# Weighted sums one step further behind the scores in the first ten units of a sigmoid-attention and top-1 MoE kernel

## The chip, the cores and the metric

The kernel runs on one core of a Trainium2 chip. The metric is the device time of one execution in microseconds (us); lower is better. Three runs of the kernel before gave 771.38 us in the median (771.14 to 772.06).

## What is computed

The reference, cut to what matters:

```python
def _attn_ref(q, k, v):                      # 8 batches, 12 heads, 448 tokens, 64 wide, float32
    scores = q @ k.transpose(0, 1, 3, 2) / sqrt(64) - log(448)
    return sigmoid(scores) @ v
def _moe_ref(x, w_gate, w1, w2):             # x: 3584 tokens x 768, 8 experts, hidden 1024
    expert_idx = argmax(x @ w_gate, axis=1)
    gate_w = softmax(x @ w_gate)[expert_idx]
    for e in range(8):
        out[mask_e] = gate_w * (relu(x[mask_e] @ w1[e]) @ w2[e])
```

## The kernel before, in words

**Units and steps.** The 48 pairs of heads (`g`; six to a batch) are taken two at a time as 24 units, `u`. A unit has seven steps, one per chunk `c` of 64 keys, and `s = 7 * u + c` counts the steps, 0 to 167. `scores(s)` (line 752) multiplies the keys of one chunk with the queries of both pairs, two heads to a pair, each head in a 64 x 64 quarter of TensorE; the result is two PSUM tiles `sc`, 128 x 448. They come from a pool of four, `ps_sc`, which is used in turn. `squash` puts the sigmoid of each into an SBUF tile `at` (eight of them) on ScalarE, line 750. `weighted(s)` (line 773) multiplies `at` with the values and adds into one PSUM tile `av` per pair over the seven steps of a unit, line 784. In the trace a float32 matmul of a quarter has two records, so the scores of one step, or its sums, are eight weight loads and eight matmuls. I call that a half-step.

**Two stages.** Up to step `START = 70` only attention runs, in rounds: each even `s` is one round, in which `weigh_to` emits some weighted sums, then the gate work that is due, then the DVE transposes of finished units (`turn_tokens`), then `score_to(s + 2)` the scores of two steps, then `copy_tokens` the ACT copies `xf` of finished units. From step 70 on, MoE matmuls (lines 243 and 266) fill the time between bursts of attention.

The rounds are these lines (948 to 955):

```python
if s % 2 == 0:
    weigh_to(min(s - 1, (done_av // ST + 1) * ST))
    if done_av and done_av % ST == 0:
        summed.setdefault(done_av // ST - 1, s)
    stages_early(s)
    turn_tokens()
    score_to(s + 2 if s else LEAD + 1)
    copy_tokens()
```

So a round never runs over the end of a unit: it has one, two or three steps of sums against two of scores.

**Gate work.** `stages_early` calls `gate_a(b)` two steps after the round in which the last unit of batch `b` was summed. `gate_a` (line 287) multiplies the six `xf` of the batch with the gate weights into `psg`, a tile of the same pool of four as the scores, and VectorE copies it out to `logits` (line 298). The fourth score tile after `psg` takes the same PSUM tile, so it waits for that copy. Later pieces (`early_b`, `early_c`, ...) stand at fixed steps; `early_c` ends in `ri`, from which SyncE (SP) reads which batch's tokens to load (`raw`, line 581).

**Into the MoE.** `SPLITS` names the steps at which the six column blocks of the first batch's tokens are split into a high and a low part on VectorE: a transpose (594), a cast (595) and a subtraction `xl` (598). `FIRST` names the steps at which the first weights are split: ScalarE casts `w1h` (161), GpSimd subtracts for `w1l` (162). `READY` turns the next keys and queries with VectorE (`turn`, 699), loads keys and values from GpSimd's queue (`load_values`, 687 and 691) and queries from SP's (667).

The order on each engine is the order in which this code emits; no scheduler moves anything here.

Of the kernel before, what the change touches and what calls it, by code (L numbers as in the profile page):

```python
# [24 lines left out]
def tile_sigmoid_attention_top1_moe(  # L25
# [263 lines left out]
    def gate_a(b):  # L289
        psg = small_ps(b, "psg")  # L290
        for t in range(KD):
            for h in range(2):
                n = t % 2 * 2 + h
                nc.tensor.matmul(
                    psg[32 * n : 32 * (n + 1), :GH], wg[:, t], wholes[b, t][:, h * GH : (h + 1) * GH],
                    start=(t < 2), stop=(t >= KD - 2),
                )
        nc.vector.tensor_copy(logits_0 if b == 0 else logits, psg[:, :GH])
# [290 lines left out]
    def split_tokens(n, t, high):  # L589

        xh = xpool.tile([P, S], F32R, tag="xh", name=f"xh_{n}_{t}")
        xl = xpool.tile([P, S], F32R, tag="xl", name=f"xl_{n}_{t}")
        whole = xpool.tile([P, S], F32, tag="whole", bufs=2, name=f"whole_{n}_{t}")
        nc.vector.transpose(whole.rearrange("p (j s) -> p j s", s=32), raws[n][:, :, t, :])
        high(xh, whole)
        low_parts.append((xl, whole, xh.bitcast(F32)))
        if n == 0:
            nc.vector.tensor_sub(*low_parts.pop())
        elif t > 0:
            nc.vector.tensor_sub(*low_parts.pop(0))  # L600
            if t == KD - 1:
                nc.vector.tensor_sub(*low_parts.pop(0))
        xch[n, t] = (xh, xl)
# [14 lines left out]
    def keep_tokens():  # L618

        while to_keep:  # L620
            b, n, xt = to_keep.pop(0)
            rows = x_tok[b * S : (b + 1) * S].rearrange("(j r) (i f) -> i r j f", r=32, i=4)
            nc.sync.nop()
            for i in range(4):
                put = nc.sync.dma_start(
                    rows[i][:, :, n * KH * 32 : (n + 1) * KH * 32],
                    xt[32 * i : 32 * (i + 1)].rearrange("r j t s -> r j (t s)"),
                )
                for got in taken:
                    tc.declare_no_dep(put.ins, got.ins, reason="the slots read earlier batches' tokens")  # L630
# [114 lines left out]
    ST = KC  # L745
# [26 lines left out]
    def weighted(s):  # L772
        u, c = divmod(s, ST)
        two = [2 * u + n for n in range(2)]
        for g in two:
            if c == 0:
                if u % 2 == 0 and s < START - ST:
                    psv[g] = ps_moe.tile([P, 512], F32, tag="moe", name=f"av_{g}")
                else:
                    psv[g] = ps_av.tile([P, 512], F32, tag="av", name=f"av_{g}")  # L780
            at = ats.pop((g, c))
            for h in range(2):
                rows = quarter(g, h)
                nc.tensor.matmul(  # L784
                    psv[g][OWN[1 - h if g == CROSS else h], :S], ops[g, "v"][rows, c, :], at[rows], start=(c == 0), stop=(c == KC - 1)
                )
        if c == KC - 1:
            for g in two:
                pv = psv.pop(g)
                if g not in BY_ROWS:  # L790
                    summed_up.append((g, pv))
                to_copy.append((g, pv))
# [4 lines left out]
    def turn_tokens():  # L797
        while summed_up:
            tokens(*summed_up.pop(0))

    def copy_tokens():
        while to_copy:
            g, pv = to_copy.pop(0)
            xf = xpool.tile([P, S], F32, tag="xf", bufs=6, name=f"xf_{g}")
            if g in BY_ROWS:
                to, frm = xf.rearrange("d (p c) -> d p c", c=KC), pv[:, :S].rearrange("d (c p) -> d p c", c=KC)
                if g == CROSS:
                    for own, other in zip(OWN, OWN[::-1]):
                        nc.vector.tensor_copy(to[own], frm[other])
                else:  # L810
                    nc.scalar.copy(to, frm)
                tokens(g, xf)
            else:
                nc.scalar.copy(xf, pv[:, :S])
            wholes[divmod(g, NP)] = xf

    WARM, K_POOL, BY_ROWS = 33, 22, (0, 1, 3)
    START = 70
    LOADS = (START - 15, START - 12, START - 9, START - 7, START - 5)
    FIRST = (START - 3, START - 1, START - 1)  # L820
    SPLITS = (START - 11, START - 10, START - 9, START - 8, START - 4, START - 3)
    PB = NP // 2 * ST
    MIX = (7, 7)

# [3 lines left out]
        2: lambda u: (turn(2 * u + 3, "k"), load_pair(2 * u + 5)),  # L828
        3: lambda u: (turn(2 * u + 3, "q"), load_values(2 * u + 3)),
    }  # L830
    BURST = 4

    def attention():

# [23 lines left out]
        done_av = done_sc = 0  # L858

        def weigh_to(n):  # L860
            nonlocal done_av
            while done_av < min(n, N_ST):
                weighted(done_av)
                done_av += 1

        def score_to(n):
            nonlocal done_sc
            while done_sc < min(n, N_ST):
                scores(done_sc)
                done_sc += 1  # L870
# [52 lines left out]
        summed = {}  # L923

        def stages_early(s):
            for b in range(B):
                if summed.get((b + 1) * NP // 2 - 1) == s - 2:
                    gate_a(b)
            for w in PLACES.get(s, ()):
                stage(*w)  # L930

        def stages_late(s):
            u, i = divmod(s, ST)
            b, r = divmod(s - PB, PB)
            if r == (BURST if b < B - 1 else 1) and (b + 1) * PB >= START:
                gate_a(b)
            for w in PLACES.get(s, ()):
                stage(*w)

        for s in range(N_ST + 11):  # L940
            u, i = divmod(s, ST)
            a = u * ST
            if s in LOADS:
                wts.load(LOADS.index(s) + 1)
            if s in FIRST:
                wts.ahead(FIRST.index(s) + 1)
            if s < START:
                if s % 2 == 0:
                    weigh_to(min(s - 1, (done_av // ST + 1) * ST))
                    if done_av and done_av % ST == 0:  # L950
                        summed.setdefault(done_av // ST - 1, s)
                    stages_early(s)
                    turn_tokens()
                    score_to(s + 2 if s else LEAD + 1)
                    copy_tokens()
            elif s == START:
                weigh_to(a)
                turn_tokens()
                score_to(a + 2)
                copy_tokens()  # L960
            yield s, MIX[0]
            keep_tokens()
            if s >= START:
                b, r = divmod(s - 3 * PB, PB)
                b += 1
                stages_late(s)
                if i == BURST:
                    for n in range(ST):
                        score_to(a + n + 3)
                        weigh_to(a + n + 1)  # L970
                        turn_tokens()
                        if n == ST - 1:
                            copy_tokens()
                        if r == PB - ST + BURST and n < KD:
                            split_tokens(b, n, nc.scalar.copy if n in (1, 4) else nc.vector.tensor_copy)
            if i in READY and s < N_ST:
                READY[i](u)
            if s in SPLITS:
                split_tokens(0, SPLITS.index(s), nc.vector.tensor_copy)
            yield s, MIX[1]  # L980
# [21 lines left out]
    for s, n in attention():  # L1002
        if s >= START:
            more(n)
# [362 lines left out]
```

## Time and profile before

| what | value |
|---|---|
| median of three runs | 771.38 us (771.14 to 772.06) |
| the profiled execution, its own time | 771.24 us |
| its span, first to last instruction | 769.4 us |
| mean granted TensorE clock | 1.00 of 2.4 GHz |
| TensorE matmul busy | 762.8 us, 99% |
| VectorE, ScalarE, GpSimd busy | 378.2, 382.2, 349.1 us |
| DMA | 125.67 MB, mean 163 GB/s |

A busy TensorE says only that a matmul is in flight; whether it goes at its full rate is seen from how many weight loads and matmuls start in a stretch. PEld is TensorE's weight-load row: it shows when each matmul's turn comes, and what it waited for. SPq and POOLq are the queues from which SyncE and GpSimd issue DMAs. In a timeline a bracket gives the idle time of that engine before the row and what ended it.

### The profile page before, as it was taken

Reading aid. Unit: us, or ns where it says so; the run is one execution under the profiler, and the core shown is the slowest. Engines: PE = TensorE matmul, PEld = TensorE weight load, DVE = VectorE, ACT = ScalarE, POOL = GpSimd, SP = SyncE. Lnnn points to the kernel's source line nnn. Section 1 sums busy time; section 2 is a strip of 40 time slices with the busy share of each in tenths; the row PEclk is TensorE's granted clock in tenths of the full one; section 3 lists DMA queues with packets and bytes.
Section 4 is the critical chain, followed back from the end, with each engine's and each line's share of the span. In section 5 each row is a group of like instructions: output and inputs, shape, how many; then the busy total and the mean of one; then the engine's idle time right before and its main releaser. Section 6 shows DMA issues by size and latency. Waiting matters only on the chain. (4 is left out here: it accounts for less than half of the span.)

```text
span 769.4 us, 15492 instructions
## 1 busy us (share of the span) xinstructions
PE 762.8 (99%) x5585; PEld 589.3 (77%) x5585; DVE 378.2 (49%) x790; ACT 382.2 (50%) x686; POOL 349.1 (45%) x342
## 2 busy tenths in 40 slices
PE   9999999999999999999999999999999999999997
PEld 5655547678687696876967769678689999999996
DVE  5433678375253751628415474244746392244443
ACT  6878676644526545364344552545523333445451
POOL 8665526245353151531705407044266654764351
PEclk9999999999999999999999999999999999999999
DMA  9786898896678665694575966566087454656671
GB/s 231 166 180 148 177 243 177 189 217 149 157 162 192 147 154 120 160 242 99 134 184 110 218 149 168 129 185 151 24 217 173 142 142 107 204 154 172 199 222 38
DMA packets 309921, 125.67 MB, mean 163 GB/s; under 512 B 208158, under 2 KB 305358, under 8 KB 309840
## 3 DMA queue, kind: packets, MB, share of 16 engines
q1 hardware_dynamic: 303632, 112.19, 61.6%
q0 software_dynamic: 5632, 11.53, 5.4%
q8 instruction: 45, 0.74, 0.5%
q10 hardware_dynamic: 576, 0.92, 0.4%
q14 instruction: 36, 0.29, 0.1%
HBM read 102.49 MB, written 22.49 MB: 162 GB/s over the span
## 5 line engine op out<-in xcount | busy, mean ns | idle before, releaser
L750 ACT ACTIVATE at<-sc,bias_s 128x448 f32<-128x448 f32 x336 | 190.7, 633 | 106.9 <-PE sc L768 106.2
L162 POOL TENSOR_TENSOR w1l<-wst,w1h 128x768 fp32r<-128x768 f32 x72 | 132.8, 1852 | 210.5 <-ACT w1h L161 207.9
L162 POOL TENSOR_TENSOR w2l<-wst,w2h 128x512 fp32r<-128x512 f32 x84 | 106.9, 1296 | 134.7 <-ACT w2h L161 134.6
L768 PE MATMUL sc<-qt,kt 64*64 64x448 f32 x1344 | 162.0, 543 | 0.0
L784 PE MATMUL av<-at,vn 64*64 64x448 f32 x1344 | 160.1, 536 | 0.0
L243 PE MATMUL ps<-xh,w1h 128*128 128x448 f32 x336 | 124.3, 370 | 0.0
L243 PE MATMUL ps<-xh,w1l 128*128 128x448 f32 x336 | 123.3, 367 | 0.0
L243 PE MATMUL ps<-xl,w1h 128*128 128x448 f32 x336 | 123.3, 367 | 0.0
L266 PE MATMUL ps<-hh,w2l 128*128 128x448 f32 x336 | 123.3, 367 | 0.0
L266 PE MATMUL ps<-hl,w2h 128*128 128x448 f32 x336 | 123.2, 367 | 0.0
L266 PE MATMUL ps<-hh,w2h 128*128 128x448 f32 x336 | 122.6, 365 | 0.0
L768 PEld LDWEIGHTS sc<-qt,kt 64*64 64x64 f32 x1344 | 75.3, 188 | 59.0 <-issue 46.5
L784 PEld LDWEIGHTS av<-at,vn 64*64 64x64 f32 x1344 | 57.5, 133 | 64.0 <-issue 53.8
L161 ACT CAST w2h<-wst 128x512 fp32r<-128x512 f32 x108 | 64.5, 620 | 75.7 <-PE ps L266 63.3
L250 ACT ACTIVATE hh<-ps 128x448 fp32r<-128x448 f32 x56 | 30.5, 545 | 138.1 <-PE ps L243 125.3
L279 DVE TENSOR_TENSOR ps<-ps,gt 128x448 f32<-128x448 f32 x42 | 40.7, 970 | 87.0 <-PE ps L266 84.7
L612 DVE STREAM_TRANSPOSE xt<-av 128x448 f32<-128x448 f32 x45 | 26.5, 626 | 95.3 <-PE av L784 95.3
L251 DVE SCALAR_TENSOR_TENSOR hl<-ps,hh 128x448 fp32r<-128x448 f32 x56 | 34.4, 614 | 76.5 <-ACT hh L250 67.0
L243 PEld LDWEIGHTS ps<-xh,w1h 128*128 128x128 f32 x336 | 63.1, 188 | 9.4 <-issue 4.4
L266 PEld LDWEIGHTS ps<-hh,w2l 128*128 128x128 f32 x336 | 65.2, 194 | 6.6 <-issue 3.5
L266 PEld LDWEIGHTS ps<-hl,w2h 128*128 128x128 f32 x336 | 65.2, 194 | 6.2 <-issue 3.2
L266 PEld LDWEIGHTS ps<-hh,w2h 128*128 128x128 f32 x336 | 65.2, 194 | 3.2
(215 smaller groups left out, 916.5 us busy)
## 6 DMA issues: line engine op xcount, KB each, us to landing
wst<-in_moe_w_dram SPq DMA_DIRECT2D x72, 384.0 KB
wst<-in_moe_w_dram SPq DMA_DIRECT2D x54, 512.0 KB
x_tok<-xt SPq DMA_DIRECT2D x64, 168.0 KB
qn<-in_q_dram SPq DMA_DIRECT2D x180, 56.0 KB
raw<-x_tok SPq DMA_DIRECT2D x28, 336.0 KB
out_dram<-ob SPq DMA_DIRECT2D x84, 112.0 KB
kn<-in_k_dram SPq DMA_DIRECT2D x104, 56.0 KB
kn<-in_k_dram POOLq DMA_DIRECT2D x76, 56.0 KB, 4.1
```

Source lines behind the costliest of these rows:

```text
L161: nc.scalar.copy(hi, st)
L162: eng.tensor_tensor(lo, st, hi.bitcast(F32), op=ALU.subtract)
L243: nc.tensor.matmul(ps[:, :S], a[:, ws], b_, start=(t == 0 and n == 0), stop=(t == KD - 1 and n == 2))
L250: nc.scalar.activation(hh[:, :S], ps[:, :S], AF.Relu)
L251: nc.vector.scalar_tensor_tensor(hl[:, :S], ps[:, :S], 0.0, hh[:, :S].bitcast(F32), op0=ALU.max, op1=ALU.subtract)
L266: nc.tensor.matmul(ps[:, :S], a, b_, start=(j == 0 and n == 0), stop=(j == KF - 1 and n == 2))
L279: nc.vector.tensor_tensor(by_gate, by_gate, gate_rows[b], op=ALU.mult)
L612: nc.vector.transpose(xts[b][:, :, t, :], pv[:, :S].rearrange("p (j s) -> p j s", s=32))
L750: nc.scalar.activation(at, ps[:, :S], AF.Sigmoid, bias=bias_s, scale=SCALE)
L768: nc.tensor.matmul(ps[quarter(g, h), :S], ks, ops[g, "q"][own], start=True, stop=True)
L784: nc.tensor.matmul(psv[g][OWN[1 - h if g == CROSS else h], :S], ops[g, "v"][rows, c, :], at[rows], start=(c == 0), stop=(c == KC - 1))
```

## The change

`BEHIND = 2` replaces the rule for the rounds before `START`: round `s` sums up to step `s - 3`, thus always the two steps `s - 4` and `s - 3`, also across the end of a unit. `summed` is filled by a loop, since the end of a unit may now lie within a round. The sixth block of tokens is split at step 68 instead of 67.

```diff
-    SPLITS = (START - 11, START - 10, START - 9, START - 8, START - 4, START - 3)
+    SPLITS = (START - 11, START - 10, START - 9, START - 8, START - 4, START - 2)
...
-    BURST = 4
+    BURST, BEHIND = 4, 2
...
-                    weigh_to(min(s - 1, (done_av // ST + 1) * ST))
-                    if done_av and done_av % ST == 0:
-                        summed.setdefault(done_av // ST - 1, s)
+                    weigh_to(s - BEHIND)
+                    while len(summed) < done_av // ST:
+                        summed[len(summed)] = s
```

What it does to the order shows at two places. The first is TensorE around `psg_2`, the gate matmuls of the third batch, at the end of the first stage (in the names the number after `sc`, `av` and `xf` is the pair, the next one the chunk). Before:

```order
L784 MATMUL av_19_1791<-at_19_1_1749,vn_19_1626 64x448 x2
L294 MATMUL psg_2_1798<-xf_12_1381,wg_98 32x224 x2
L294 MATMUL psg_2_1798<-xf_13_1383,wg_98 32x224 x2
L294 MATMUL psg_2_1798<-xf_14_1603,wg_98 32x224 x2
L294 MATMUL psg_2_1798<-xf_15_1605,wg_98 32x224 x2
L294 MATMUL psg_2_1798<-xf_16_1761,wg_98 32x224 x2
L294 MATMUL psg_2_1798<-xf_17_1763,wg_98 32x224 x2
L768 MATMUL sc_18_3_1812<-qt_18_1570,kt_18_1558 64x448 x2
L768 MATMUL sc_19_3_1813<-qt_19_1624,kt_19_1612 64x448 x2
L768 MATMUL sc_18_4_1822<-qt_18_1570,kt_18_1558 64x448 x2
L768 MATMUL sc_19_4_1823<-qt_19_1624,kt_19_1612 64x448 x2
```

and with the change:

```order
L784 MATMUL av_19_1780<-at_19_2_1753,vn_19_1626 64x448 x2
L294 MATMUL psg_2_1839<-xf_12_1457,wg_98 32x224 x2
L294 MATMUL psg_2_1839<-xf_13_1459,wg_98 32x224 x2
L294 MATMUL psg_2_1839<-xf_14_1603,wg_98 32x224 x2
L294 MATMUL psg_2_1839<-xf_15_1605,wg_98 32x224 x2
L294 MATMUL psg_2_1839<-xf_16_1805,wg_98 32x224 x2
L294 MATMUL psg_2_1839<-xf_17_1807,wg_98 32x224 x2
L768 MATMUL sc_18_5_1853<-qt_18_1566,kt_18_1554 64x448 x2
L768 MATMUL sc_19_5_1854<-qt_19_1624,kt_19_1612 64x448 x2
L768 MATMUL sc_18_6_1863<-qt_18_1566,kt_18_1554 64x448 x2
L768 MATMUL sc_19_6_1864<-qt_19_1624,kt_19_1612 64x448 x2
```

`psg_2` now stands after the scores of steps 0 to 67 and the sums of 0 to 65, where it stood after 0 to 65 and 0 to 64: three half-steps later. In both, the built program makes the last score tile shown (`sc_19_4`, now `sc_19_6`), the fourth behind `psg_2`, wait for VectorE.

The second place is VectorE at the same time, from the turn of pair 20's keys on. Before:

```order
L699 STREAM_TRANSPOSE kt_1719<-kn_1560 128x448
L612 STREAM_TRANSPOSE xt_1_1581<-av_1635 128x14x32
L612 STREAM_TRANSPOSE xt_1_1581<-av_1638 128x14x32
L699 STREAM_TRANSPOSE qt_1770<-qn_1565 128x448
L699 STREAM_TRANSPOSE kt_1776<-kn_1614 128x448
L298 COPY logits<-psg_1798 128x224
L699 STREAM_TRANSPOSE qt_1832<-qn_1619 128x448
L594 STREAM_TRANSPOSE whole_4_1839<-raw_1429 128x448
L595 CAST xh_4_1837<-whole_4_1839 128x448
L598 TENSOR_TENSOR xl_4_1838<-whole_4_1839,xh_4_1837 128x448
```

and with the change:

```order
L699 STREAM_TRANSPOSE kt_1715<-kn_1556 128x448
L699 STREAM_TRANSPOSE qt_1755<-qn_1561 128x448
L699 STREAM_TRANSPOSE kt_1761<-kn_1614 128x448
L612 STREAM_TRANSPOSE xt_1_1581<-av_1635 128x14x32
L612 STREAM_TRANSPOSE xt_1_1581<-av_1638 128x14x32
L699 STREAM_TRANSPOSE qt_1814<-qn_1619 128x448
L594 STREAM_TRANSPOSE whole_4_1821<-raw_1418 128x448
L595 CAST xh_4_1819<-whole_4_1821 128x448
L598 TENSOR_TENSOR xl_4_1820<-whole_4_1821,xh_4_1819 128x448
L298 COPY logits<-psg_1839 128x224
```

The copy of `psg` stood ahead of the turn of pair 21's queries and of the split of the fifth token block; now both stand ahead of it.

## Rows read from the trace of the kernel before

**Rows 1.** The page, part 1: engines' busy time, share, instructions.
```profile
PE 762.8 (99%) x5585; PEld 589.3 (77%) x5585; DVE 378.2 (49%) x790; ACT 382.2 (50%) x686; POOL 349.1 (45%) x342
```
**Rows 2.** Busy time by stretch; in brackets the instructions; at the end clock, DMA share, GB/s.
```profile
43.80:76.90 33.10, 33.10 (x354) 17.26 (x352) 11.15 (x20) 26.31 (x49) 18.32 (x31) 1.00 0.74 160
86.00:110.10 24.10, 24.10 (x256) 12.39 (x256) 22.05 (x73) 19.24 (x38) 12.48 (x21) 1.00 0.98 207
```
**Rows 3.** Waits of PEld from 6 to 121 us: total, times, longest.
```profile
PEld av L784 <- ACT at L750: 7.2, 33, 0.3
PEld sc L768 <- ACT at L750: 3.5, 19, 0.2
PEld psg L294 <- issue: 2.1, 3, 0.7
```
**Rows 4.** Timeline of PEld from 108 us: start, length, operation, count, idle before.
```profile
109.81 0.14 PEld L784 LDWEIGHTS av<-at,vn 64*64 64x64 f32 x2 [0.24 <-issue]
110.65 0.91 PEld L294 LDWEIGHTS psg<-xf,wg 128*32 128x32 f32 x24 [0.70 <-issue]
111.92 0.33 PEld L768 LDWEIGHTS sc<-qt,kt 64*64 64x64 f32 x8 [0.36 <-issue]
112.41 0.58 PEld L768 LDWEIGHTS sc<-qt,kt 64*64 64x64 f32 x8 [0.17 <-issue]
...
117.80 0.72 PEld L784 LDWEIGHTS av<-at,vn 64*64 64x64 f32 x8 [0.33 <-ACT at L750]
...
120.73 0.19 PEld L243 LDWEIGHTS ps<-xh,w1h 128*128 128x128 f32 x1 [0.65 <-issue]
```
**Rows 5.** Timeline of VectorE, 106 to 119.5 us.
```profile
107.48 0.63 DVE L598 TENSOR_TENSOR xl<-whole,xh 128x448 fp32r<-128x448 f32 x1
...
112.06 0.39 DVE L298 COPY logits<-psg 128x224 f32<-128x224 f32 x1 [1.29 <-PE psg L294]
114.59 0.65 DVE L699 STREAM_TRANSPOSE qt<-qn 128x448 f32<-128x448 f32 x1 [2.13 <-DMA qn<-in_q_dram]
...
116.22 2.16 DVE L598 TENSOR_TENSOR xl<-whole,xh 128x448 fp32r<-128x448 f32 x1
118.30 0.63 DVE L594 STREAM_TRANSPOSE whole<-raw 128x448 f32<-128x448 f32 x1
...
119.39 2.12 DVE L598 TENSOR_TENSOR xl<-whole,xh 128x448 fp32r<-128x448 f32 x1
```
**Rows 6.** Timeline of ScalarE, 105 to 119.5 us.
```profile
108.19 2.21 ACT L750 ACTIVATE at<-sc,bias_s 128x448 f32<-128x448 f32 x4 [0.80 <-PE sc L768]
110.27 0.98 ACT L814 COPY xf<-av 128x448 f32<-128x448 f32 x2
...
115.14 0.85 ACT L161 CAST w1h<-wst 128x768 fp32r<-128x768 f32 x1
```
**Rows 7.** Timeline of GpSimd, 107 to 121 us.
```profile
107.64 0.56 POOL L687 DMA_DIRECT2D vn<-in_v_dram  x1 [5.61 <-PE av L784]
...
116.08 1.81 POOL L162 TENSOR_TENSOR w1l<-wst,w1h 128x768 fp32r<-128x768 f32 x1 [6.83 <-ACT w1h L161]
```
**Rows 8.** Timeline of SP's queue, 102 to 112 us.
```profile
107.16 2.33 SPq L667 DMA_DIRECT2D qn<-in_q_dram  x4
```
**Rows 9.** Timeline of VectorE, 85 to 92 us.
```profile
86.32 1.17 DVE L612 STREAM_TRANSPOSE xt<-av 128x448 f32<-128x448 f32 x2
87.42 0.22 DVE L361 TENSOR_REDUCE early_h<-early_l 128x16 f32<-128x64 f32 x1
```
**Rows 10.** Busy time by stretch, as rows 2; the DMA share is last but one.
```profile
91.00:93.50 2.50, 2.50 (x32) 1.42 (x28) 2.29 (x11) 1.70 (x4) 1.89 (x4) 1.00 0.61 148
93.50:98.00 4.50, 4.50 (x52) 2.39 (x46) 3.95 (x23) 3.70 (x8) 0.14 (x1) 1.00 1.12 229
```
**Rows 11.** Timeline of VectorE, 20 to 60 us: the copy of the first `psg`.
```profile
43.96 0.39 DVE L298 COPY early_l<-psg 128x224 f32<-128x224 f32 x1 [2.59 <-PE psg L294]
```
**Rows 12.** Waits of PEld from 121 to 770 us, the longest that is not issue.
```profile
PEld sc L768 <- ACT xh L595: 2.0, 9, 0.2
```

## The prediction

> **What bounds the kernel now.** I read the page first: TensorE is busy 99% of the span [rows 1], so only TensorE's own time counts. Busy does not mean full rate, so the next view is the count of weight loads by stretch. Between the gate works of batches 0 and 1 the PEld column has 352 loads in 33.10 us, which is 44 half-steps of 8 loads at 0.752 us; later 256 in 24.10 us, 32 half-steps at 0.753 us [rows 2]. The reader should see that two stretches with rounds of one, two and three steps of sums have the same rate to 0.2%: the uneven rounds cost nothing. The waits of PEld say the same in another way. Before the first MoE matmul the sums wait for the sigmoid 33 times and the scores 19 times, but none of these waits is over 0.3 us [rows 3], and they lie in the gap of about 0.2 us that PEld has before every group of four loads while the previous matmuls stream. After that stage the longest-lived wait that is not issue comes to 2.0 us in 640 us [rows 12]; so what TensorE loses before step 70 is not made up later, and what it gains is kept.
>
> What the first stage does lose is at the gate work: TensorE's loads pause 0.70 us before `psg` and 0.36 us after it [rows 4], a change of tile shape that the change leaves as often as it was.
>
> **The change part by part.**
>
> *Sums one step further behind, rounds of two.* The number of matmuls is the same. The sums get 1.5 us more before they need a sigmoid, but the sigmoid was already in time, so I cost this at a gain of at most what the longest of these waits shows: 0.33 us against the usual 0.20, at the three-step round of step 70 [rows 4]; I take 0.15 us. The cover is the eight `at` tiles: the sigmoid of step `s` writes the tiles of step `s - 4`, whose sums now stand in the same round ahead of the scores of `s`, so it does not wait.
>
> *Gate work, value loads and token stores, at unit ends up to two half-steps later.* On GpSimd's queue the value loads wait for the end of a unit (5.61 us the last time [rows 7]) and now issue up to 1.5 us later; they are wanted most of a unit after, so nothing waits. On SP's queue the store of batch 2's second half moves behind a weight load and the loads of pair 23; it is read only after step 70. The first `psg` is copied behind one more turn of queries, but VectorE stood idle 2.59 us ahead of that copy [rows 11]: nothing.
>
> *The third `psg` and its copy.* This is the one place with a price. `psg_2` moves three half-steps later: 3 x 0.752 = 2.26 us. Its loads start at 110.65 + 2.26 = 112.91, its product is there for VectorE at 112.06 + 2.26 = 114.32 [rows 4, 5], and the fourth score tile behind it, whose load began about 112.41 + 0.38 = 112.79 before, is wanted at 115.05. That tile needs the PSUM that `psg` leaves, thus the copy. In the kernel before the copy ran on an idle VectorE and was over at 112.45, so TensorE saw nothing. Now two things stand ahead of it on VectorE.
>
> The first is the turn of pair 21's queries, which waited 2.13 us for its DMA, until 114.59 [rows 5]. When will it be there now? `early_c` starts one half-step earlier and loses two token transposes of 1.10 us (86.32 to 87.42 [rows 9]) from its chain to `ri`, so the load of `raw` starts 0.75 + 1.10 = 1.85 us earlier. The DMA engines had a share of 0.61 until 93.5 us and 1.12 from there on [rows 10]; filling 1.85 us of the first kind brings all that is queued behind forward by 1.85 x (1.12 - 0.61) / 1.12 = 0.84 us, to 113.75. The value loads issued at 107.64 [rows 7], which share the engines with these queries (issued from 107.16 on [rows 8]), come 1.5 us later and may give them as much again: 112.9. I take the middle, 113.3; the bounds are 112.2 (both, with half a microsecond more) and 114.59 (neither).
>
> The second is the split of the fifth token block. From the start of the turn to the start of its subtraction `xl` it is 116.22 - 114.59 = 1.63 us, so 114.93. The subtraction took 0.63 us for the fourth block, 2.16 us for the fifth, because GpSimd's `w1l` had begun 0.14 us ahead of it and ran until 117.89; `xl` ended 0.49 us after that [rows 5, 7]. Where is `w1l` now? The scores behind which the sigmoids and the copies of unit 8 run move three half-steps: sigmoids at 108.19 + 2.26 = 110.45, copies 2.08 later at 112.53, the cast `w1h` behind them at about 113.45 and over at 114.30 (0.85), `w1l` from 114.39 to 116.20 (1.81) [rows 6, 7]. It begins before `xl` does, so `xl` ends at 116.20 + 0.49 = 116.69, the copy starts 0.08 us ahead of that end, as the next VectorE row did (118.30), and is over at 116.61 + 0.39 = 117.00. TensorE stands from 115.05 to 117.00: **1.95 us**. Were the queries as late as before, `xl` would start at 116.22, behind `w1l`, and the copy end at 117.16: 2.1 us. The price hardly depends on when they come, unless `xl` gets ahead of `w1l`.
>
> *The sixth split one step later.* It now comes behind the copy: over about 119 us, or 2 us later if the next `w1l` is ahead of it; before, it ended at 121.51 [rows 5], and the MoE began at 120.73 [rows 4] with this block its last to be read. Nothing.
>
> *Sum.* 1.95 for the copy, less 0.15 to 0.25 for the short wait of step 70 and for a load that can run ahead of its matmul: **+1.75 us**. On the profiled execution that is 771.24 + 1.75 = 772.99; the median lies 0.14 higher, so 773.1. By itself this case spans 772.7 to 773.6.
>
> **The rivals.** The first is mine: the copy is held until `w1l` is through, 773.1. 0.51.
>
> *The queries land early; not slower.* If the turn starts before 112.76 (114.39 - 1.63), `xl` is ahead of `w1l`, takes the 0.63 us of the fourth block, and the copy is over at about 115.0: no stall, and 0.15 us gained, 771.2. For it: the two shifts above, both at their full size, reach 112.9 and with a little more 112.2. Against it: the later value loads would still meet the last of these queries. That `xl` is not slowed by a `w1l` that comes second is shown by no row; the price lies between 0 and the 1.75 us of the first case, and I take 0, as the row of 0.63 us is the nearest one for an undisturbed start. 0.34.
>
> On this the Trainium skill (SBUF — State Buffer, section SBUF: two separate sides) has a rule: the SBUF port pair of VectorE and GpSimd is an exclusive lock, held by whichever instruction begins first for its whole length while the other is blocked altogether. By it the stall of this case is exactly nothing; if the two shared the ports instead, it would be up to 1.75 us. The trace agrees for the order that it shows, 2.16 us for an `xl` that came second; no row shows the other order.
>
> *The lead removes real waits; faster.* If the 7.2 and 3.5 us of waits on the sigmoid [rows 3] were lost time, up to 10.7 us would come back: 760.7; a quarter of it gives 768.7. Against it stands the even rate of rows 2, in which these waits lie. 0.07.
>
> *The queries land later than before; much slower.* The turn is the head of VectorE's queue, so past 114.59 each microsecond is a microsecond of TensorE: one gives 771.38 + 2.1 + 1.0 = 774.5. For it: DMA at its limit there, at a share of 1.12 [rows 10]. Against it: nothing is put ahead of them. 0.08.
>
> That the change does not do what it says can be left out: the built order shows both moves.
>
> **How the numbers follow.** A measurement of this kernel can tell about 0.2%, 1.54 us, from no change, so slower begins at 772.92. Of the 0.51 some 0.08 falls below that. Slower: 0.43 + 0.08 = 0.51. Same: 0.34 + 0.08 = 0.42. Faster: 0.07. The range takes in the early case with a little gain, 771.0, and the first case with its upper bound and some noise, 773.9; outside lie the two cases of 0.07 and 0.08. The likeliest time is that of the first case, 773.1.
>
> **What would show it.** In the profile of the changed kernel: a wait of a score load on VectorE's `logits` of nearly 2 us, some 2 us after the third `psg`, and the first MoE load about 1.75 us after 120.73; the copy directly behind an `xl` of over a microsecond that ends half a microsecond after `w1l`; `raw` issued about 1.85 us earlier; the rate between the gate works still 0.752 us; the waits of the sums on the sigmoid mostly gone. The prediction is wrong if the copy ends by 115.05, if the stretches of rows 2 get shorter by more than 0.3 us, or if TensorE waits anywhere else before the MoE.

## The result, and the profile after

The changed kernel takes **775.45 us** (median of 6 runs, 773.86 to 776.64) against 771.46 for the kernel before (6 runs, 771.07 to 772.06): a ratio of 1.0051, with a 95% interval of 1.0038 to 1.0064. It is slower, as forecast, but by 4.0 us instead of 1.75, and above the range, which ended at 773.9.

The profiled execution is the shortest of the six, 773.86 us. Busy time in the page, part 1, as in [rows 1]:

```profile
PE 765.0 (99%) x5585; PEld 587.7 (76%) x5585; DVE 376.5 (49%) x790; ACT 383.0 (50%) x686; POOL 349.1 (45%) x342
```

TensorE's busy time grew by 2.2 us with the same 5585 instructions, so again the waits have to be read from PEld. The waits of PEld from 6 to 125 us (total, times, longest):

```profile
PEld av L784 <- issue: 23.1, 114, 0.2
PEld sc L768 <- issue: 13.1, 64, 1.0
PEld sc L768 <- ACT at L750: 3.8, 18, 0.7
...
PEld av L784 <- DMA vn<-in_v_dram: 1.2, 2, 1.0
...
PEld av L784 <- ACT at L750: 0.4, 2, 0.2
```

The waits of the sums on the sigmoid are down to 0.4 us from 7.2 in [rows 3], but the pauses themselves are not gone. They are only named otherwise, as this row of the kernel before (6 to 121 us) shows:

```profile
PEld av L784 <- issue: 16.0, 81, 0.2
```

With the sigmoid's, that was 16.0 + 7.2 = 23.2 us of short pauses ahead of sums, and it is 23.1 + 0.4 = 23.5 now. Beside them stand three new waits that are far longer than the 0.2 us of a group of four: 1.0 and 0.7 us ahead of score loads, and 1.0 us ahead of sums, for a transfer of `vn`. There is no wait on `logits`. The timeline of PEld shows where they lie:

```profile
7.29 0.21 PEld L768 LDWEIGHTS sc<-qt,kt 64*64 64x64 f32 x8
...
14.49 0.63 PEld L768 LDWEIGHTS sc<-qt,kt 64*64 64x64 f32 x8
16.10 0.35 PEld L768 LDWEIGHTS sc<-qt,kt 64*64 64x64 f32 x8 [0.99 <-issue]
...
28.42 0.72 PEld L768 LDWEIGHTS sc<-qt,kt 64*64 64x64 f32 x10 [0.70 <-ACT at L750]
...
101.78 0.19 PEld L784 LDWEIGHTS av<-at,vn 64*64 64x64 f32 x2 [1.01 <-DMA vn<-in_v_dram]
...
115.86 0.92 PEld L294 LDWEIGHTS psg<-xf,wg 128*32 128x32 f32 x24 [0.70 <-ACT at L750]
...
123.37 0.19 PEld L243 LDWEIGHTS ps<-xh,w1h 128*128 128x128 f32 x1 [0.65 <-issue]
```

The first MoE load comes at 123.37 instead of 120.73 [rows 4], 2.64 us later, and the two profiled executions differ by 773.86 - 771.24 = 2.62: all of the difference lies ahead of the MoE. Of it, 0.83 us are a later start of this execution (first scores at 7.29, and at 6.46 before), which has nothing to do with the change; the last section comes back to it.

```profile
6.46 0.21 PEld L768 LDWEIGHTS sc<-qt,kt 64*64 64x64 f32 x8
```

From the first score load to the first MoE load it is 116.08 us here and 114.27 before. These 1.81 us are what the change cost in this execution. I had not costed a wait before 110 us at all.

**What the scores wait for at 16.10 and 28.42.** VectorE's timeline of the changed kernel:

```profile
15.38 0.60 DVE L699 STREAM_TRANSPOSE qt<-qn 128x448 f32<-128x448 f32 x1
...
25.18 0.65 DVE L612 STREAM_TRANSPOSE xt<-xf 128x448 f32<-128x448 f32 x1 [7.13 <-ACT xf L811]
25.84 1.26 DVE L809 COPY xf<-av 64x448 f32<-64x448 f32 x2
27.13 0.65 DVE L612 STREAM_TRANSPOSE xt<-xf 128x448 f32<-128x448 f32 x1
27.70 0.60 DVE L699 STREAM_TRANSPOSE qt<-qn 128x448 f32<-128x448 f32 x1
```

The loads at 16.10 are the first scores of unit 1. They follow the turn of pair 2's queries, over at 15.38 + 0.60 = 15.98, and the row of TensorE's matmuls names that turn:

```profile
16.13 1.03 PE L768 MATMUL sc<-qt,kt 64*64 64x448 f32 x8 [0.24 <-DVE qt L699]
```

With one step of sums fewer ahead of them these scores come a half-step (0.752 us) earlier in TensorE's order, and the turns do not. In the kernel before, that turn ended at 15.18 and the loads began at 15.19, so there was nothing to spare:

```profile
14.58 0.60 DVE L699 STREAM_TRANSPOSE qt<-qn 128x448 f32<-128x448 f32 x1
...
15.19 0.57 PEld L768 LDWEIGHTS sc<-qt,kt 64*64 64x64 f32 x8 [0.21 <-issue]
```

The loads at 28.42 are the first scores of pair 5, in unit 2. They follow the turn of pair 5's queries, over at 28.30. That turn stands behind the copies and transposes of pairs 0 and 1, which begin at 25.18 here and began at 21.50 before, because the sums of unit 0 end one round later than they did:

```profile
21.50 0.65 DVE L612 STREAM_TRANSPOSE xt<-xf 128x448 f32<-128x448 f32 x1 [5.08 <-ACT xf L811]
```

**What the sums wait for at 101.78.** The value loads of pairs 16 and 17 take the buffers of pairs 12 and 13, which come free at the end of unit 6. GpSimd's timeline, before:

```profile
86.19 0.57 POOL L687 DMA_DIRECT2D vn<-in_v_dram  x1 [5.16 <-PE pc L351]
...
89.28 1.08 POOL L691 DMA_DIRECT2D vn<-in_v_dram  x2
```

and after:

```profile
89.83 0.57 POOL L687 DMA_DIRECT2D vn<-in_v_dram  x1 [6.91 <-PE av L784]
...
92.92 1.08 POOL L691 DMA_DIRECT2D vn<-in_v_dram  x2
```

They issue 3.64 us later. The sums that want them stand where they stood in TensorE's order and are late by some 1.7 us only (the loads of `ones` for batch 0's counts start at 86.82 for 85.84, one half-step earlier in the order). So 1.9 us of the time that the transfers had are gone, but that is the smaller part: the two transfers of pair 17 (line 691) also take longer to land. The first profile has no landing for them; other profiles have. Issues from 85 to 95 us, the last figure being the median from issue to landing, in the third profile of the changed kernel (run 11):

```profile
vn<-in_v_dram POOLq DMA_DIRECT2D x2, 112.0 KB, 8.5
```

and in run 3, in which unit 6 ends where it ended before the change:

```profile
vn<-in_v_dram POOLq DMA_DIRECT2D x2, 112.0 KB, 2.3
```

In run 3 they are issued at 89.82, ahead of the loads of `raw`, which begin at 91.75; in the third profile at 92.06, behind those loads, which begin at 90.45. So these 8.5 us, and not only the later issue, make them land after they are due. That it is `raw` that they then share the DMA engines with (a share of 1.12 from 93.5 us on in [rows 10]) is likely, but no run moves `raw` alone. The values of pair 16, issued earlier, land in time.

**The copy of the third `psg`, in this execution.** VectorE:

```profile
114.91 0.65 DVE L699 STREAM_TRANSPOSE qt<-qn 128x448 f32<-128x448 f32 x1 [2.00 <-DMA qn<-in_q_dram]
...
116.55 0.63 DVE L598 TENSOR_TENSOR xl<-whole,xh 128x448 fp32r<-128x448 f32 x1
117.28 0.39 DVE L298 COPY logits<-psg 128x224 f32<-128x224 f32 x1
```

Here `xl` took 0.63 us and the copy came as soon as `psg` was there. This is my rival of the early queries. TensorE is late by 115.86 - 112.91 = 2.95 us at the third `psg` against my forecast of its place. Less this delay the turn starts at 114.91 - 2.95 = 111.96, under the 112.76 below which I let that rival hold.

### The profile page after: what moved, and what is told of

It is laid out like the page before. It is cut to its first block, busy times and chain, and to the rows that moved or that the text cites. A ratio compares the mean times of both kernels' runs of the same rounds, so it can differ in the third digit from the quotient of the medians.

```text
span 772.0 us, 15492 instructions
## 1 busy us (share of the span) xinstructions
PE 765.0 (99%) x5585; PEld 587.7 (76%) x5585; DVE 376.5 (49%) x790; ACT 383.0 (50%) x686; POOL 349.1 (45%) x342
```

## The experiments

My theory on record (A): the copy of the third `psg` is held, about 2 us. Two rivals from the profile: (B) the first units' scores come ahead of VectorE's turns, about 1 us; (C) the values of pairs 16 and 17 are issued late and those of pair 17 land late, about 1 us. The runs below are measured together with runs of the kernel before, whose medians were 771.50, 771.55 and 771.65.

**1. One step behind.** Only the crossing of unit ends and the later sixth split are left.

```diff
-    BURST, BEHIND = 4, 2
+    BURST, BEHIND = 4, 1
```

> The changed kernel with the sums one step behind the scores as before, so that only the crossing of unit ends (and the sixth split) is left of the change. On record: my forecast put the price at the third `psg`, which here stands within a row of where it stood before the change; then 771.4. The second theory (the first scores of units 1 and 2 come ahead of VectorE's turns because a step of sums fewer stands before them) also gives 771.4, since that step of sums is back. The third theory (a unit's sums that end a round later hold the value buffers, so that the value loads of pairs 16 and 17 land late) gives 771.4 too, as the odd unit ends are back where they were. If instead rounds that cross a unit end cost by themselves, over 772.5.

770.91 us (11 runs), ratio 0.9991 (0.9983 to 1.0). Rounds that cross unit ends cost nothing; all of the loss comes with the second step of lag. The waits of PEld in this run, from 6 to 121 us:

```profile
PEld av L784 <- ACT at L750: 14.8, 70, 0.3
```

Twice the waits on the sigmoid of the kernel before [rows 3], and not a slower kernel: these waits are not lost time.

**2. The old start.** The rule of before until step 16.

```diff
-                    weigh_to(s - BEHIND)
+                    weigh_to(min(s - 1, (done_av // ST + 1) * ST) if s < 16 else s - BEHIND)
```

> The changed kernel with the rule of before for the sums until step 16, the change's rule from there on. The changed kernel's trace shows score loads that stand 0.99 us ahead of 16.10 and 0.70 us ahead of 28.42, and the first `psg` 1.06 us late beside what the later start and the order explain. If the first units' turns are the cause, 775.45 - 1.06 = 774.4, and both pauses are gone. If the price is the copy of the third `psg`, 775.45 as the changed kernel.

774.43 us (5 runs), ratio 1.0036 (1.0023 to 1.0049): 1.0 us less, as B has it, and both pauses are gone. But A is in this profile too:

```profile
PEld sc L768 <- DVE logits L298: 2.0, 1, 2.0
...
PEld av L784 <- DMA vn<-in_v_dram: 0.9, 2, 0.6
```

**3. The old start and the old end of unit 6.**

```diff
-                    weigh_to(min(s - 1, (done_av // ST + 1) * ST) if s < 16 else s - BEHIND)
+                    weigh_to(min(s - 1, (done_av // ST + 1) * ST) if s < 16 else s - 1 if s == 50 else s - BEHIND)
```

> As the run with the old start, and at step 50 the sums go up to the end of unit 6 as they did before the change, so that the value buffers of pairs 12 and 13 come free 1.5 us earlier. If the late value loads are a cause (TensorE waited 1.0 and 0.2 us for `vn` at 101.78 and 102.19), 1.2 us less than the run before it: 773.2. If the copy of the third `psg` is the price, no change: 775.45.

773.60 us (8 runs), ratio 1.0030 (1.0019 to 1.004): 0.83 us less, for 1.2 expected from the first profile and 0.9 from that of run 2. Its profile has no wait on `vn`, and 2.25 us on `logits`.

**4. Also the old end of unit 8,** which moves the third `psg` back.

```diff
-                    weigh_to(min(s - 1, (done_av // ST + 1) * ST) if s < 16 else s - 1 if s == 50 else s - BEHIND)
+                    weigh_to(min(s - 1, (done_av // ST + 1) * ST) if s < 16 else s - 1 if s in (50, 64) else s - BEHIND)
```

> As the run before it, and at step 64 the sums go up to the end of unit 8, which moves the third `psg` from half-step 134 to 130 of the order, ahead even of the 131 of the kernel before the change. If the copy of that `psg` behind VectorE's turn and split costs 1.95 us in most executions (in the one profile of the changed kernel it did not), 771.3. If only the start and the values cost, 773.2 as the run before it.

772.00 us (11 runs), ratio 1.0006 (0.9997 to 1.0015): 1.6 us less and no wait on `logits`, but 0.7 short of the expected 771.3. A part of the rest is in its waits of PEld: this `psg` came so early that it waited for ScalarE's copies of the tokens.

```profile
PEld psg L294 <- ACT xf L814: 0.7, 2, 0.4
```

**5. The changed kernel again.**

> The changed kernel once more, for a second profile. In its first profile the copy of the third `psg` held nobody, but that execution was the shortest of six, 1.6 us under their median. If the missing 1.6 us are the wait of the scores on VectorE's `logits` (2.04 and 2.25 us in the profiles of the runs with the old start and with unit 6), a profile of about 775.4 shows that wait at some 2 us beside the two waits of the first units. If the profile is of 775 or more without it, the missing time is somewhere else.

775.30 us (5 runs), ratio 1.0055 (1.0041 to 1.0068), so the result repeats. The profiled execution was again the shortest, 773.20, with the waits of B and C and none on `logits`. That left open whether A is in the longer ones.

**6. Run 3 with the fifth and sixth splits after the copy.**

```diff
-    SPLITS = (START - 11, START - 10, START - 9, START - 8, START - 4, START - 2)
+    SPLITS = (START - 11, START - 10, START - 9, START - 8, START - 2, START - 1)
```

> As the run with the old start and unit 6 (773.6; its profile has 2.25 us of wait on `logits`), with the splits of the fifth and sixth token blocks after the copy of the third `psg`: at steps 68 and 69 of the order instead of 66 and 68. On record I said that the copy is held by the turn of pair 21's queries and by the split. In that profile the turn starts at 115.39, the split's first instruction at 115.95, the copy at 117.56: without the split the copy comes 1.61 us earlier, 773.6 - 1.6 = 772.0, and 0.6 us of wait are left, for the queries. If the queries alone held the copy, 773.6 as before; if it isn't the copy at all, also 773.6.

771.51 us (11 runs), ratio 1.000 (0.9991 to 1.001): 2.1 us less than run 3, more than the 1.6 expected, since the wait for the queries that I left in it is not in its profile. VectorE there:

```profile
113.87 0.65 DVE L699 STREAM_TRANSPOSE qt<-qn 128x448 f32<-128x448 f32 x1 [3.11 <-DMA qn<-in_q_dram]
114.44 0.35 DVE L298 COPY logits<-psg 128x224 f32<-128x224 f32 x1
```

The copy stands directly behind the turn. With the start, unit 6 and this split undone, the kernel is back at the time before.

**7. Two steps behind in the middle only,** from step 16 to 47.

```diff
-                    weigh_to(s - BEHIND)
+                    weigh_to(s - (2 if 16 <= s < 48 else 1))
```

> The sums two steps behind the scores only from step 16 to 47, one step behind elsewhere, crossing unit ends all along. By all three causes (first units, values of unit 6, third `psg`) nothing is left to pay: as the run with one step behind throughout, 770.9. If a lag of two steps costs by itself in steady running (the run with three places undone stood 1.1 us over the one with one step), up to 771.9.

770.92 us (11 runs), ratio 0.9996 (0.9987 to 1.0005): as run 1. To within the 0.7 us that the interval leaves, the lag by itself neither costs nor gives anything in these steps.

**8. Only the even rounds:** run 1 with the sixth split where it was.

```diff
-    SPLITS = (START - 11, START - 10, START - 9, START - 8, START - 4, START - 2)
+    SPLITS = (START - 11, START - 10, START - 9, START - 8, START - 4, START - 3)
```

> One step behind, crossing unit ends, and the sixth split where it stood before the change: of the change, only the even rounds are left. If the 0.6 us by which the run with one step behind was under the kernel before come from the even rounds, 770.9 again; if they come from the later sixth split, 771.5. On record both were costed at nothing, which is 771.4.

771.28 us (11 runs), ratio 0.9997 (0.9988 to 1.0006). It lies between the two expectations, and its interval overlaps that of run 1 for the most part: by the times it is not settled whether the even rounds or the split give a few tenths. The profiles speak for the even rounds: from the first score load to the first MoE load it is 113.69 us in run 1 and 113.68 in run 8, whose splits differ, and 114.27 in the kernel before, one profile each. So the even rounds may give 0.6 us, where I had 0.15, and the split nothing. No version here is clearly under the kernel before; run 1 comes nearest.

**9. The changed kernel with only the splits moved,** the edit of run 6.

> The changed kernel, only with the splits of the fifth and sixth token blocks after the copy of the third `psg` (steps 68 and 69 of the order, for 66 and 68). With the old start and unit 6 this took 2.1 us off (773.60 to 771.51). If the copy costs the changed kernel as much in most of its executions, 775.4 - 2.1 = 773.3. If its two profiles, without that wait, are typical, about 775.4 as without the edit, and the missing 1.6 to 2.2 us are somewhere that no profile has shown.

773.59 us (9 runs), ratio 1.0027 (1.0018 to 1.0037): 1.7 to 1.9 us less than the changed kernel, so A is in most of its executions. Its profile has the waits of B and C and none on `logits`.

**10. The old end of unit 0 only.**

```diff
-                    weigh_to(s - BEHIND)
+                    weigh_to(s - 1 if s == 8 else s - BEHIND)
```

> The changed kernel, only that at step 8 the sums go up to the end of unit 0 as before the change, so that the copies and transposes of pairs 0 and 1 stand ahead of the turn of pair 5's queries a round earlier. If the pause ahead of 28.42 comes from that turn standing behind them (VectorE: transposes and copies 25.18 to 27.70, the turn 27.70 to 28.30), it goes and the pause ahead of 16.10 stays: 775.4 less 0.5 (0.70 us against the 0.2 that every group of four has), 774.9. If both pauses come from a step of sums fewer ahead of the scores, 775.4.

774.50 us (5 runs), ratio 1.0040 (1.0026 to 1.0054). The pause at 28 us is gone, that of unit 1 stays:

```profile
15.44 0.34 PEld L768 LDWEIGHTS sc<-qt,kt 64*64 64x64 f32 x8 [1.08 <-ACT at L750]
```

So the two pauses have different causes, as expected. The time fell by 0.8 to 0.95 instead of 0.5, to that of run 2, which undoes both. The profiles part the two better than these medians: from the first score load to the first MoE load it is 117.66 us here, 116.81 in run 2, and 118.04 and 118.11 in the two profiles of the changed kernel that come next, which have the wait A as these two have. So the pause of unit 2 is worth about 0.4 us, and both together 1.2 to 1.3.

**11 and 12. Two more profiles of the changed kernel.**

> The changed kernel for a third profile. If it is of about 775.4, it has the wait on `logits` of some 2 us. If it is again of about 773.5, it has the waits of the first units and of `vn` and none on `logits`.

> The changed kernel for a fourth profile, with the same two cases as the third: about 775.4 with a wait on `logits` of some 2 us, or about 773.5 without it.

774.93 and 775.89 us, one execution each, and both have the wait. The third profile, waits of PEld:

```profile
PEld sc L768 <- DVE logits L298: 2.0, 1, 2.0
...
PEld av L784 <- DMA vn<-in_v_dram: 1.0, 2, 0.7
```

Its timeline of all engines (here VectorE, GpSimd and the score load that waits):

```profile
114.86 0.65 DVE L699 STREAM_TRANSPOSE qt<-qn 128x448 f32<-128x448 f32 x1 [2.51 <-DMA qn<-in_q_dram]
115.43 0.60 DVE L594 STREAM_TRANSPOSE whole<-raw 128x448 f32<-128x448 f32 x1
116.06 1.80 POOL L162 TENSOR_TENSOR w1l<-wst,w1h 128x768 fp32r<-128x768 f32 x1 [3.63 <-ACT w1h L161]
116.07 2.05 DVE L595 CAST xh<-whole 128x448 fp32r<-128x448 f32 x1
118.16 0.62 DVE L598 TENSOR_TENSOR xl<-whole,xh 128x448 fp32r<-128x448 f32 x1
118.70 0.38 DVE L298 COPY logits<-psg 128x224 f32<-128x224 f32 x1
...
119.13 0.20 PEld L768 LDWEIGHTS sc<-qt,kt 64*64 64x64 f32 x2 [2.03 <-DVE logits L298]
```

This is the chain of the forecast link by link: the turn waits for its queries, the split stands behind it, one of its instructions waits until `w1l` is through, the copy comes last, and the fourth score tile waits for the copy.

The fourth profile has the same wait, 2.04 us, with less of `w1l` in it. The queries come later there (the turn starts at 117.03, last section) and the cast takes 0.69 us for the 0.39 that it takes alone, where it took 2.05 in the third: 0.30 us lost to `w1l` against 1.66. In run 3, with 2.25 us of wait, the cast loses nothing. So in these two executions late queries and the split behind them hold the copy nearly or quite as long without `w1l`. Moving `w1l` alone, which no run does, would by these rows not have freed it every time.

Whether the wait is there goes with the queries, as the forecast has it. In the four profiles the turn starts at 114.91, 113.46, 114.86 and 117.03, and the third `psg` at 115.86, 115.17, 114.77 and 115.56 for the 112.91 of the forecast. Less that delay the turns are at 111.96, 111.20, 113.00 and 114.38, and only the two above 112.76 have the wait. What makes the queries land so differently is not shown. From the first score load to the first MoE load the four take 116.08, 116.07, 118.04 and 118.11 us, two and two, the wait apart; the kernel before took 114.27. Of the 13 executions of the changed kernel the two whose profiles lack that wait are the shortest, 773.20 and 773.86; all others took 774.93 or more, though nine of these have no profile.

## Why the prediction was wrong in size

**The copy of the third `psg`: right.** Forecast 1.95 us; measured 2.03 and 2.04 in two profiles of the changed kernel, and 1.7 to 2.1 by taking the split away. Set back by TensorE's delay at that `psg` (114.77 in the third profile, 1.86 over the forecast 112.91), the turn starts at 113.0 and the copy ends at 119.08 - 1.86 = 117.2; I had said 113.3 and 117.00. One link differs: it was the cast `xh` that waited for `w1l`, not `xl`. That the price hardly depends on when the queries come, unless they come early, held as well. So the way that the time moved was no luck, though it would have come out the same without this wait: run 9, which has only the other two costs, is at 773.59.

**The rival of the early queries: right too, as the rarer case.** Two of four profiles show it. In them `xl` was over when `w1l` began, to 0.02 us, so they do not tell whether a `w1l` that comes second slows it. Run 1 does: `xl` begins 0.35 us ahead of `w1l` and takes its usual 0.63 us, and `w1l` takes 1.96 us for 1.81.

```profile
115.60 0.63 DVE L598 TENSOR_TENSOR xl<-whole,xh 128x448 fp32r<-128x448 f32 x1
115.95 1.96 POOL L162 TENSOR_TENSOR w1l<-wst,w1h 128x768 fp32r<-128x768 f32 x1 [6.71 <-ACT w1h L161]
```

So taking 0 for that price was right. In the third profile `w1l` came first: the cast began 0.01 us after it and took 2.05 us, to 0.26 us past its end, against 0.39 us elsewhere. Both orders agree with the rule of the Trainium skill (SBUF — State Buffer, section SBUF: two separate sides) that, for the kinds of VectorE instruction that use the port pair shared with GpSimd, whichever of the two starts first has it for its whole instruction and the other is blocked.

**Value loads at unit ends: the first step that failed.** I wrote that they "are wanted most of a unit after, so nothing waits". I had the time at which they are wanted, but not the one at which they land: I took no issue-to-landing time from the trace and put no DMA share beside it, though I used that share (1.12 [rows 10]) for the queries that come later. Issued a round later, those of pair 17 took 8.5 us to land instead of 2.3, and the sums waited for them. Cost: 0.83 us (run 3 against run 2).

**The start: the second step that failed, by not being there.** I took the even rate of [rows 2] as proof that nothing waits, and these stretches begin at 43.80 us. Units 1 and 2 have their turns made just ahead of use; the lag brings the scores forward as much as it puts the sums back, and I followed only the sums. I had also said that a unit's end may come later at no cost, and here VectorE's copies for unit 0 pushed a turn. Cost: 1.0 us (run 2). My last sign of being wrong, that TensorE waits anywhere else before the MoE, came true with these two steps.

The sum of the three, 771.46 + 1.0 + 0.83 + 2.0 = 775.3, is the measured 775.45 within its spread, and runs 2, 3 and 6, which undo them one after the other, end at 771.51.

**Nothing from the removed waits, and nothing for the later sixth split: right.** Run 7 against run 1 (770.92 and 770.91), of which only the latter has the sums one step behind in the middle, shows the first; runs 1 and 8, with intervals that overlap, show no price for the second. The load of `raw` was to start 1.85 us earlier; it started at 91.31 for 91.26, in an execution whose TensorE was by then some 1.7 us late, so that the shift was there, and this delay (the later start of the execution and the pauses of units 1 and 2) had used it up.

## What to carry to other kernels

A lag between two stages moves both: list what each side needs and when, at the ends of the pipeline first, where there is no steady rate to read it from. A buffer that is held one round longer delays the transfer into it, and that transfer's landing, with what is issued ahead of it, is what must be compared with its use. A wait that changes its name in the profile while the pauses stay as long is no gain. And when one profile is the shortest of its runs, look at a second: what it lacks may be what most executions pay.

## What was not expected of the hardware

*The start varies between executions by 0.8 us.* The first score loads came at 6.46 us in the profile before and at 7.29, 6.60, 6.56 and 7.29 in the four of the changed kernel, though the order up to there is the same. The matmuls that turn the first queries, by source line, before and in the fourth profile of the changed kernel (least, median and greatest ns, first and last start):

```profile
L714 PE MATMUL turn_q<-ident,qn x56: 218/218/267, 4.6 to 5.4; 64*64 64x64 f32 x56
```

```profile
L714 PE MATMUL turn_q<-ident,qn x56: 311/311/366, 4.7 to 6.1; 64*64 64x64 f32 x56
```

The same 56 matmuls have a median of 218 or 311 ns. What goes with it is the granted clock. The trace's record of the granted clock begins, with 1.00 (2.4 GHz), at 4.13 us in the profile before and at 6.60, 4.80, 4.69 and 6.83 us in the four; ahead of it there is no record, and a window there reads 1.00 only for want of one. In all fourteen profiles of this case TensorE runs matmuls from 1.04 us on, and these small ones take about 311 ns until that record begins and 218 ns from there on. The first score load comes at 6.43 to 6.60 us in the five where it begins before 4.9 us, and at 7.24 to 7.29 in the five where it begins after 6.1. This is a spread of every kernel here, and not of the change.

*Not every instruction of VectorE waits for `w1l`.* In the fourth profile the transposes beside it took 0.65 and 0.60 us, as they do alone, and the cast behind them waited:

```profile
116.85 1.82 POOL L162 TENSOR_TENSOR w1l<-wst,w1h 128x768 fp32r<-128x768 f32 x1 [3.64 <-ACT w1h L161]
117.03 0.65 DVE L699 STREAM_TRANSPOSE qt<-qn 128x448 f32<-128x448 f32 x1 [3.80 <-DMA qn<-in_q_dram]
117.59 0.60 DVE L594 STREAM_TRANSPOSE whole<-raw 128x448 f32<-128x448 f32 x1
118.23 0.69 DVE L595 CAST xh<-whole 128x448 fp32r<-128x448 f32 x1
```
